# Weights laid side by side in the prologue of an attention and state-space kernel

## The chip, the cores and the metric

The kernel runs on one core of one Trainium2 chip. The metric is the device time of one execution, in microseconds (us). TensorE (PE) multiplies, VectorE (DVE), ScalarE (ACT) and GpSimd (POOL) do the element-wise work, and SyncE (SP) issues nearly all transfers.

## The reference

Two independent halves are computed and set side by side in the output. Half A is a state-space layer over a sequence of 2048 steps with 640 channels; half B is attention with 32 query heads of 20 elements that share one key head and one value head.

```
B:  q = (x @ wq) in 32 heads of 20     k = x @ wk      v = x @ wv
    p = softmax(q k^T / sqrt(20))      b = (p v, heads joined) @ wo
A:  h[t] = Lam_bar * h[t-1] + x[t] @ B_bar^T           (complex, 640 states)
    a = 2 Re(h @ C^T) + x * Dskip
out = concatenate([a, b])              x is (1, 2048, 640), bfloat16
```

## The kernel before, in words

**Tiling.** The scores of one head group (4 heads), one block of 512 queries and one chunk of 128 keys make a tile of 128 keys by 512 queries; there are 4 query blocks x 8 head groups x 16 key chunks x 4 heads = 2048 such tiles. A score tile is one product with a contraction over 32 rows (20 elements of the head, one row that carries a bound, the rest zero). Its exponential is made in one of two ways. ACT exponentiates two or three tiles in one instruction (line 1457, out tile PR, shapes 128x1024 and 128x1536). Or DVE turns one tile into the bits of a bfloat16 number by an addition and a conversion to integers (line 862, out tile BIG, 128x512), and three more integer additions, on DVE (line 862, BIG from BIG) or on POOL (line 1772, two tiles at once), make shifted copies of it that take part in the weighted sum too. The sums over keys (MB from PR,VP and MB from BIG,VS) are PE products of 32 columns each, four of them beside one another in the four column strips of the array.

**Order.** Nothing of the order is written by hand. `Schedule` (line 46) is a list scheduler that runs while the program is built: each step has an engine, a planned duration, dependences and a priority, and whichever ready step has the lowest priority number goes next on its engine. Sources such as `fill` (line 1394) and `pv_source` (line 1785) decide at the planned time which tile goes to ACT and which to DVE. `planned` (line 505) makes 32 such plans with small random shifts, and keeps the one that it believes shortest. So a changed duration, priority or step early in the program changes what is decided later, up to the end. `Emitter.plan` (line 271) then turns dependences into semaphore waits. Each engine runs its own stream strictly in order.

**The prologue** ends when the first exponential starts on ACT. Its steps:

- `loads` (line 1013): SP issues, in this order, the first two blocks of B's x (tile CT), the first 80 columns of wq, three transposing loads of the third and fourth block of x into BIG (tile xbT in the code; the fourth block in two parts of 3 and 2 chunks), wv, the rest of wq, and the two matrices B_re and B_im (tile BA, 800 KB each). wk goes out on ACT's queue.
- `kv_steps` (line 1094): `turn` transposes the first two blocks on PE (line 725, SC from ident,CT), and DVE or ACT copies the result to BIG (lines 1110 and 1113). `kv` makes the keys of each of the four blocks `tb`. The 20 columns of wk are wanted in four copies, one for each of the four row groups of the score product, so each of the 5 chunks of the contraction is multiplied four times by the same 32 columns, once for each column strip (`four`, line 1227): 20 products of 128x32 weights per block, tile wkr. DVE then takes the largest absolute value of each row (line 1130, tile mab), and ACT copies the keys to KT (line 1136).
- `bound` (line 1154): from the maxima of the first three blocks DVE makes `Mp` (lines 1156 and 861); when the fourth arrives, one combined instruction makes M0 (line 1161, tile M). The maximum over all four (line 1164) goes to DRAM (mrep, line 705) and comes back spread over the partitions (mcol); DVE then makes Mm from it (line 857), from which the bounds of the remaining head groups come.
- `qt_task` (line 1235) makes the queries of the first head group: a first product with zeros (MB from PR,VZ) and then, for each of 5 chunks, four products of 20 columns of wq (MB from BIG). ACT copies them to QT (line 1252), DVE takes absolute values (line 861), a product with M0 adds the bound (MB from BIG,M), and DVE writes QT again (line 862, QT from MB,lift). Then the first scores can be made.
- `warm_source` (line 933) fills idle time of PE in the prologue with products of zeros (MB from PR).

**Just after the start**, PE makes the rest of the queries (line 795, SC from BIG) and values (`v_task`, line 1183: lines 1187 and 1195) in banks that are lent by the two sets of three score banks (SC0, SC1). DVE, in its stream order, copies these, scales the state-space matrices (BA, CA), waits for mcol, and makes Mm. Until a lent bank has been emptied by DVE, the set that lent it can't take its third tile.

Of the kernel before, what the change touches and what calls it, by code (L numbers as in the profile page):

```python
# [12 lines left out]
ALU = mybir.AluOpType  # L13
AX = mybir.AxisListType
FP32 = mybir.dt.float32
BF16 = mybir.dt.bfloat16
# [449 lines left out]
class Build:  # L466
# [191 lines left out]
    def alloc_early(self, s):  # L658
        self.maskM = self.sb(s, "maskM", [128, NC, 32], FP32)
        self.mask0 = self.sb(s, "mask0", [128, 4, 32], FP32)  # L660
        self.Mp = self.sb(s, "Mp", [128, 4, 32], FP32)
# [6 lines left out]
        self.EARLY = ["iota", "one", "vrow", "maskM", "mask0", "Mp", "turn2", "angc"] + [f"early_fr{c}{i}" for c in range(NC) for i in range(2)]  # L668

# [348 lines left out]
    def loads(self):  # L1018
# [23 lines left out]
        self.wq_op = L(wqd[:, :, 80:640], wqv[:, :, 80:640], 380000, "wq", strided=True, writes=["wqb"])  # L1042
        for o, t in zip(self.vec_op + self.xn_op + [self.wk_op, self.wqa_op, self.wv_op, self.wq_op], self.LANDS):
            o.lands = t
# [54 lines left out]
    def kv_steps(self):  # L1099
# [20 lines left out]
        def kv(tb):  # L1120
            yield lambda: all((tb, c) in self.xb_op for c in range(NC)) and (tb < self.PLAIN or self.s.done([self.xb_op[tb, 0]])) \
                and any(x in self.early for x in self.free_banks)
            bank = self.take(self.early)
            prev = None
            for c in range(NC):
                prev = self.pe(self.four(bank, [p.wkr[:, c, :]] * 4, p.xbT[:, c, 512 * tb:512 * tb + 512], c == 0, c == NC - 1),
                               self.mmt(512), mode="C", prio=self.KP if tb < 3 else 1.15,
                               deps=[self.xb_op[tb, c], self.wk_op] + bank.last, prev=prev,
                               reads=[f"xbT{tb}_{c}", "wkr"], writes=[bank.key])
            red = self.dve(lambda e, src=bank.ap: e.tensor_reduce(out=p.mab[:, tb:tb + 1], in_=src, axis=AX.X, op=ALU.max,  # L1130
                                                     apply_absolute_value=True), 650, deps=[prev], reads=[bank.key],
                           writes=[f"mab{tb}"], prio=0.31)
            self.red_op[tb] = red
            dst, src = p.KT[:, 512 * tb:512 * tb + 512], bank.ap
            if self.KEYS[tb] == "a":
                kt = self.act(lambda e: e.activation(dst, src, ACT.Identity, bias=p.lift[:, 2:3], scale=ALPHA * UNIT), 600,
                              deps=[red, self.lift_op], reads=[bank.key, "lift"], writes=[f"KT{tb}"], prio=0.34)
            else:
                kt = self.dve(self.ts(dst, src, ALPHA * UNIT, p.lift[:, 2:3], ALU.mult, ALU.add), 640,
                              deps=[red, self.lift_op], reads=[bank.key, "lift"], writes=[f"KT{tb}"], prio=0.44)  # L1140
            self.kt_op[tb] = kt
            yield lambda: kt.start is not None
            bank.last = [kt]
            self.give(bank)
            if tb < 2:
                yield lambda: any(x in self.early for x in self.free_banks)
                yield from self.v_task(tb, self.take(self.early))
# [6 lines left out]
        def bound():  # L1154
            yield lambda: set(range(3)) <= set(self.red_op)
            most = self.dve(lambda e: e.tensor_reduce(out=p.mab[:, 6:7], in_=p.mab[:, 0:3], axis=AX.X, op=ALU.max), 120,
                            deps=[self.red_op[i] for i in range(3)], reads=[f"mab{i}" for i in range(3)], writes=["mabp"], prio=0.32)
            low = self.dve(self.ts(p.Mp[:], p.mask0[:], p.mab[:, 6:7], None, ALU.mult), 200, port=True,
                           deps=[most, self.c_op["mask0"]], reads=["mabp", "mask0"], writes=["Mp"], prio=0.32)
            yield lambda: len(self.red_op) == 4  # L1160
            self.m0_op = self.dve(lambda e: e.scalar_tensor_tensor(out=p.M0[:], in0=p.mask0[:], scalar=p.mab[:, 3:4], in1=p.Mp[:],
                                                                   op0=ALU.mult, op1=ALU.min), 250,
                                  deps=[self.red_op[3], low, self.c_op["mask0"]], reads=["mab3", "Mp", "mask0"], writes=["M0"], prio=0.3)
            m = self.dve(lambda e: e.tensor_reduce(out=p.mab[:, 4:5], in_=p.mab[:, 0:4], axis=AX.X, op=ALU.max), 120,
                         deps=[self.red_op[3]], reads=[f"mab{i}" for i in range(4)], writes=["mabs"],
                         prio=0.36)
            many = bass.AP(tensor=p.mab, offset=4, ap=[[8, DH], [0, H], [1, 1]])
            out = self.load(p.mrep.rearrange("(h d o) -> d h o", d=DH, o=1), many, 2560, "mo", strided=True, deps=[m], reads=["mabs"],
# [38 lines left out]

    def take(self, which=None):
        for b in self.free_banks:
# [17 lines left out]
    def four(self, bank, lhs, rhs, start, stop):  # L1227

        return [self.mm(bank.tensor[32 * j:32 * j + lhs[j].shape[-1], bank.off:bank.off + 512], lhs[j], rhs, start, stop,
                        tile_position=(0, 32 * j), skip_group_check=True) for j in range(4)]  # L1230

    def first_made(self):
        return (0, -1) in self.half_op and self.half_op[0, -1][0].start is not None

    def qt_task(self, bank, g=0):

        p = self
        rank = self.QR if g == 0 else 1.3
        prev = self.pe(self.four(bank, [p.VZ[:]] * 4, p.PR[:, 0, :] if g == 0 else p.KT[:, 0:512], True, False), self.mmt(512),
                       deps=[self.c_op["VZ"], self.zero_op] + bank.last + ([self.kt_op[0]] if g else [self.wqa_op]), prio=rank, mode="C",  # L1240
                       reads=["VZ", "KT0" if g else "PR0"], writes=[bank.key])
        for c in range(NC):
            at = 640 * c + 80 * g
            prev = self.pe(self.four(bank, [p.wqf[:, at + 20 * j:at + 20 * j + 20] for j in range(4)], p.xbT[:, c, 0:512],
                                     False, c == NC - 1), self.mmt(512), deps=[self.wqa_op, self.wq_op][:g + 1] + [self.xb_op[0, c]],
# [793 lines left out]
    def ssm_scalars(self):  # L2039
# [23 lines left out]
        def ts(o, a, s1, s2, op0, op1=None):  # L2063
# [7 lines left out]
        w = self.pe([self.mm(bank.cols(16, 16 + NC), p.vrow[:], p.ident[0:4 * NC, 3 * NC:4 * NC], True, True)], 80.0,  # L2071
                    deps=[self.vec_op[3], v, chain[0]], reads=["ident"] + [f"vrow{i}" for i in range(4)], writes=[bank.key], prio=1.06)
        skip = self.dve(lambda e: e.tensor_copy(sc[:, 3, :], bank.cols(16, 16 + NC)), 150, deps=[w], reads=[bank.key], writes=["scd"],
# [35 lines left out]
        for lo, hi in ((0, 3), (3, NC)):  # L2109
            keys = [f"early_fr{c}{i}" for c in range(lo, hi) for i in range(2)]  # L2110
            t = self.act(lambda e, lo=lo, hi=hi: e.activation(p.tab[:, lo:hi, 1:3, :], p.fr[:, lo:hi].bitcast(I16)[:, :, :, 0::2], ACT.Sin,
                                                              scale=TWO_PI / 65536.0), 200 + 427 * (hi - lo), table="sin",
                         deps=turns[2 * lo:2 * hi] + [sin_table], reads=keys, writes=[f"tab{c}" for c in range(lo, hi)], prio=0.4, gate=self.turned)
            tabs += [t] * (hi - lo)
# [438 lines left out]
```

## Time and profile before

| what | value |
|---|---|
| median of 3 runs (lowest, highest) | 710.6 us (709.87, 711.77) |
| time of the profiled execution | 711.06 us |
| its span on the core | 709.2 us |
| ACT busy | 693.6 us |
| PE busy | 688.4 us |
| DVE busy | 610.4 us |
| POOL busy | 467.3 us |
| first exponential starts on ACT | 19.15 us |

The profiled execution's own time is 1.86 us longer than its span; this stands before the first and behind the last instruction. Busy time of PE is modelled from overlapping products and is no measure of how much room PE has. In lines of groups the columns are: line, engine, operation, output from inputs, shapes and count; then busy time and mean duration of one in ns; then idle time of the engine before them and what ended it.

### The profile page before, as it was taken

How to read it: one execution, taken by the hardware profiler on the slowest of the kernel's cores; microseconds unless marked ns; L12 is line 12 of the kernel's file. 1: busy time of each engine (PE TensorE's matmuls, PEld its weight loads, DVE VectorE, ACT ScalarE, POOL GpSimd, SP SyncE). 2: the span in 40 equal slices, each digit the busy share in tenths (PEclk: the TensorE clock that was granted, in tenths of full speed). 3: DMA queues.
4: the chain of work that ended last, by engine and by line, in shares of the span. 5: the costliest groups of instructions: out<-in, count | busy, mean ns of one | idle time of the engine just before them, and what ended most of it. 6: DMA issues, size and time to landing. Idle time of an engine off the chain costs nothing.

```text
span 709.2 us, 26838 instructions
## 1 busy us (share of the span) xinstructions
PE 688.4 (97%) x11287; PEld 246.0 (35%) x11287; DVE 610.4 (86%) x1168; ACT 693.6 (98%) x703; POOL 467.3 (66%) x796
## 2 busy tenths in 40 slices
PE   8999999999999999999999999999999999999997
PEld 4322323434333533333433333334233333342323
DVE  7899899987897788888789999889999997987783
ACT  6899999999999999999999999999999999999996
POOL 4255673046697566955757776967867777798881
PEclk9999999999999999999999999999999999999999
DMA  9687652120120000100301000120000001110001
GB/s 208 152 170 164 139 106 78 37 48 11 27 66 10 21 21 22 50 22 17 65 10 37 19 18 25 49 61 20 10 17 20 14 25 31 31 28 16 26 15 39
DMA packets 77588, 34.44 MB, mean 49 GB/s; under 512 B 58350, under 2 KB 77470, under 8 KB 77470
## 3 DMA queue, kind: packets, MB, share of 16 engines
q1 hardware_dynamic: 76506, 32.44, 19.8%
q8 instruction: 90, 1.47, 0.9%
q10 hardware_dynamic: 964, 0.29, 0.2%
q14 instruction: 28, 0.23, 0.1%
HBM read 11.53 MB, written 9.75 MB: 30 GB/s over the span
## 4 chain that ended last, share of the span: by engine, by line
ACT 49%; PE 44%; DMA 3%; DVE 2%; SPq 1%; issue 0%; DVEq 0%
ACT PR L1457 49%; PE MB L725 17%; PE MB L795 11%; PE SC L725 11%; PE MB L805 4%; DMA mrep<-mab 2%; SPq L710 1%; DMA BIG<-in_B_x_dram 1%; DVE BIG L862 1%; PE MB L721 1%; DMA mcol<-mrep 1%; PE SC L721 0%; DMA qd<-BIG 0%; SPq L706 0%; DVE prod L857 0%
## 5 line engine op out<-in xcount | busy, mean ns | idle before, releaser
L1457 ACT ACTIVATE PR<-SC 128x1024 bf16<-128x1024 f32 (+1 forms) x681 | 679.4, 1197 | 4.0 <-PE SC L725 2.8
L1772 POOL INT64_ADD BIG<-BIG x762 | 455.4, 614 | 214.3 <-DVE BIG L862 118.7
L862 DVE TENSOR_SCALAR BIG<-SC 128x512 int16<-128x512 f32 x529 | 356.3, 685 | 67.7 <-PE SC L725 60.8
L725 PE MATMUL SC<-QT,KT 32*128 32x512 bf16 x2013 | 266.4, 384 | 10.3 <-ACT PR L1457 5.2
L725 PE MATMUL MB<-BIG,VS 128*32 128x512 bf16 x2256 | 247.8, 384 | 0.3 <-DVE pvsb L1839 0.2
L725 PE MATMUL MB<-PR,VP 128*32 128x512 bf16 x1484 | 204.9, 384 | 0.0
L725 PEld LDWEIGHTS SC<-QT,KT 32*128 32x128 bf16 x2013 | 68.1, 90 | 174.2 <-ACT PR L1457 113.1
L725 PEld LDWEIGHTS MB<-BIG,VS 128*32 128x32 bf16 x2256 | 59.1, 94 | 61.4 <-issue 39.1
L725 PEld LDWEIGHTS MB<-PR,VP 128*32 128x32 bf16 x1484 | 49.9, 94 | 49.5 <-issue 36.5
L795 PE MATMUL MB<-CT,W 128*32 128x320 bf16 (+2 forms) x1000 | 53.4, 301 | 0.4 <-DVE prod L857 0.2
L805 PE MATMUL MB<-xaT,BT 32*128 32x256 bf16 x184 | 35.6, 272 | 1.6 <-ACT PR L1457 1.4
L862 DVE TENSOR_SCALAR BIG<-BIG 128x1024 int16<-128x1024 int16 (+1 forms) x91 | 34.7, 410 | 2.6 <-PE MB L725 2.3
L795 PE MATMUL MB<-CA,W 128*32 128x512 bf16 (+1 forms) x640 | 35.2, 302 | 0.3 <-DVE prod L857 0.2
L795 PE MATMUL MB<-xaT,BA 128*32 128x256 bf16 x800 | 32.0, 275 | 0.1
L805 PE MATMUL MB<-diagD,xaT 32*128 32x128 bf16 x320 | 31.3, 217 | 0.0
L795 PEld LDWEIGHTS MB<-CT,W 128*32 128x32 bf16 x1000 | 22.8, 96 | 15.2 <-issue 6.6
L805 PEld LDWEIGHTS MB<-diagD,xaT 32*128 32x128 bf16 x320 | 17.7, 92 | 28.4 <-ACT PR L1457 20.4
L795 PE MATMUL MB<-xaT,BT 128*32 128x256 bf16 x616 | 26.1, 274 | 0.0
L857 DVE TENSOR_TENSOR prod<-MB,tab 128x1024 bf16<-128x1024 f32 x20 | 24.3, 1215 | 0.5 <-PE SC L725 0.5
L2024 DVE CAST stg<-MB 128x512 bf16<-128x512 f32 x35 | 23.8, 679 | 1.1 <-PE MB L795 0.8
L862 DVE TENSOR_SCALAR BIG<-MB 128x512 int16<-128x512 f32 x35 | 23.8, 680 | 0.0
L795 PE MATMUL MB<-WO,OP 128*32 128x128 bf16 (+1 forms) x480 | 23.5, 302 | 0.0
(167 smaller groups left out, 469.5 us busy)
## 6 DMA issues: line engine op xcount, KB each, us to landing
out_dram<-stg SPq DMA_DIRECT2D x31, 128.0 KB, 1.9
qd<-BIG SPq DMA_DIRECT2D x20, 128.0 KB, 2.2
QT<-qd SPq DMA_DIRECT2D x28, 80.0 KB
OP<-pvsb SPq DMA_DIRECT2D x105, 20.0 KB
rdP<-recs SPq DMA_DIRECT2D x105, 20.0 KB
lbd<-BA SPq DMA_DIRECT2D x5, 320.0 KB, 3.3
CT<-in_B_x_dram SPq DMA_DIRECT2D x2, 640.0 KB, 5.3
BA<-in_A_B_re_dram SPq DMA_DIRECT2D x1, 800.0 KB, 7.1
```

The lines of the kernel that those rows point to most:

```text
L710: fns = [lambda e, o=o, i=i: e.dma_start_transpose(o, i) for o, i in pairs]
L721: r = e.matmul(out[32 * j:32 * j + 32], lhsT=lhsT[:, 32 * j:32 * j + 32], rhs=rhs, start=start, stop=stop, tile_position=(0, 32 * j), skip ...
L725: return lambda e: e.matmul(out, lhsT=lhsT, rhs=rhs, start=start, stop=stop, **kw)
L795: x = e.matmul(out[32 * j:32 * j + 32], lhsT=lhsT[:, 32 * j:32 * j + 32], rhs=rhs, start=start, stop=r.end is tag, tile_position=(0, 32 * ...
L805: return lambda e: e.matmul(out, lhsT=lhsT[at], rhs=rhs[at], start=False, stop=r.end is tag, tile_position=(32 * row, 0), skip_group_check ...
L857: return lambda e: e.tensor_tensor(out, a, b, op)
L862: return lambda e: e.tensor_scalar(out, a, s1, s2, op0=op0, op1=op1)
L1457: ex = self.act(lambda e: e.activation(dst, t[:, 0:512 * n], ACT.Exp, scale=1.0 / UNIT), 0.8333 * 512 * n + 64, table="exp", deps=[op], re ...
L1772: op.fns.append(lambda e: e.int64_add(words(dst), words(src), add))
L2024: ev = self.dve(lambda e: e.tensor_copy(st, bank.ap), 645, deps=[prev], reads=[bank.key], writes=[key], prio=self.EV, gate=(lambda: last.e ...
```

## The change

Three things are changed in the prologue, with the constants that belong to them.

1. **Weights side by side.** POOL copies wk's padded 32 columns four times beside one another into a new tile `wks` (128 columns per chunk), and the 80 columns of wq of the first head group into `wqp` with 12 zeros between the heads (DVE clears the tile first). For the second, third and fourth block one product with 128 columns then makes what four products with 32 columns made; for the first head group's queries too, without the first product with zeros. The first block keeps its four products (`QUAD_KEYS = 1`).
2. **Last keys in halves.** The fourth block is multiplied in two halves of 256 columns, in the order `KEY_STEPS`: chunks 0 to 2 of both halves (they land first), then chunks 3 and 4 of the one half and of the other. Each half has its own maximum.
3. **The bound as one maximum and one product.** `Mp` and the combined instruction go; DVE takes the maximum of the five maxima and multiplies the mask by it.

Priorities of the key products, of the sine and of one small product are changed, the first block's keys are copied by DVE in place of ACT, and the banks of the prologue are taken in a given order (`KEY_BANKS`).

```diff
+        again = bass.AP(tensor=p.wkr, offset=0, ap=[[NC * 32, 128], [32, NC], [0, 4], [1, 32]])
+        spread = p.wks[:].rearrange("p (c j n) -> p c j n", c=NC, j=4)
+        self.wks_op = self.pool(lambda e: e.tensor_copy(spread, again), 800, deps=[self.wk_op], reads=["wkr"], writes=["wks"],
+                                prio=self.WKP, port=True)
...
+        zero = self.dve(lambda e: e.memset(p.wqp[:], 0.0), 170, writes=["wqp"], prio=0.65)
+        self.wqp_op = self.pool(lambda e: e.tensor_copy(padded, dense), 600, deps=[zero, self.wqa_op], ...)
...
-    PLAIN, KP, QR, FRP = 2, 1.1, 1.12, 0.36
-    TURNED, KEYS = ("dadad", "dadad"), "aaaa"
+    PLAIN, KP, QR, FRP, SINP, SKIP_P, KEY_BANKS = 2, (1.04, 1.04, 1.06, 1.08), 1.05, 0.36, 0.32, 1.03, "2543016"
+    WKP, QUAD_KEYS = 0.9, 1
+    TURNED, KEYS = ("dadad", "dadad"), "daaa"
...
-            for c in range(NC):
-                prev = self.pe(self.four(bank, [p.wkr[:, c, :]] * 4, p.xbT[:, c, 512 * tb:512 * tb + 512], c == 0, c == NC - 1),
+            parts = 1 if tb < 3 else 2
+            n = 512 // parts
+            steps = [(x, c) for x in range(parts) for c in range(NC)] if tb < 3 else self.KEY_STEPS
+            for x, c in steps:
+                at = 512 * tb + n * x
+                if tb < self.QUAD_KEYS:
+                    prev = self.pe(self.four(bank, [p.wkr[:, c, :]] * 4, p.xbT[:, c, at:at + 512], c == 0, c == NC - 1), ...
+                else:
+                    prev = self.pe([lambda e, x=x, c=c, at=at: e.matmul(bank.cols(n * x, n * x + n), lhsT=p.wks[:, 128 * c:128 * c + 128],
+                                                                        rhs=p.xbT[:, c, at:at + n], start=c == 0, stop=c == NC - 1, ...
+                if c == NC - 1:
+                    red = self.dve(... tensor_reduce(out=to, in_=src, axis=AX.X, op=ALU.max, apply_absolute_value=True), 115 + 1.05 * n, ...
...
-            low = self.dve(self.ts(p.Mp[:], p.mask0[:], p.mab[:, 6:7], None, ALU.mult), 200, port=True, ...
-            self.m0_op = self.dve(lambda e: e.scalar_tensor_tensor(out=p.M0[:], in0=p.mask0[:], scalar=p.mab[:, 3:4], in1=p.Mp[:],
-                                                                   op0=ALU.mult, op1=ALU.min), 250, ...
+            yield lambda: len(self.red_op) == 5
+            m = self.dve(lambda e: e.tensor_reduce(out=p.mab[:, 5:6], in_=p.mab[:, 0:5], axis=AX.X, op=ALU.max), 120, ...
+            self.m0_op = self.dve(self.ts(p.M0[:], p.mask0[:], p.mab[:, 5:6], None, ALU.mult), 200, port=True, ...
...
+    KEY_STEPS = ((0, 0), (0, 1), (0, 2), (1, 0), (1, 1), (1, 2), (0, 3), (0, 4), (1, 3), (1, 4))
...
+            if g == 0:
+                prev = self.pe([lambda e, c=c: e.matmul(bank.ap, lhsT=p.wqp[:, 128 * c:128 * c + 128], rhs=p.xbT[:, c, 0:512], ...
```

More of the change, by code (lines that the diff above doesn't have):

```diff
@@ L667, in alloc_early @@
         self.vrow = self.sb(s, "vrow", [20, 128], BF16)
-        self.EARLY = ["iota", "one", "vrow", "maskM", "mask0", "Mp", "turn2", "angc"] + [f"early_fr{c}{i}" for c in range(NC) for i in range(2)]
+        self.wqp = self.sb(s, "wqp", [128, NC * 128], BF16)
+        self.wks = self.sb(s, "wks", [128, NC * 128], BF16)
+        self.EARLY = ["iota", "wqp", "wks", "one", "vrow", "maskM", "mask0", "turn2", "angc"] + [f"early_fr{c}{i}" for c in range(NC) for i in range(2)]
     def alloc_late(self, s):
@@ L1122, in kv @@
                 and any(x in self.early for x in self.free_banks)
[L1123 removed]
+            bank = self.take(self.early, self.KEY_BANKS)
             prev = None
[L1125 to L1129 removed]
@@ new lines, in kv @@
+            for x, c in steps:
+                at = 512 * tb + n * x
+                if tb < self.QUAD_KEYS:
+                    prev = self.pe(self.four(bank, [p.wkr[:, c, :]] * 4, p.xbT[:, c, at:at + 512], c == 0, c == NC - 1), self.mmt(512),
+                                   mode="C", prio=self.KP[tb], deps=[self.xb_op[tb, c], self.wk_op] + bank.last, prev=prev,
+                                   reads=[f"xbT{tb}_{c}", "wkr"], writes=[bank.key])
+                else:
+                    prev = self.pe([lambda e, x=x, c=c, at=at: e.matmul(bank.cols(n * x, n * x + n), lhsT=p.wks[:, 128 * c:128 * c + 128],
+                                                                        rhs=p.xbT[:, c, at:at + n], start=c == 0, stop=c == NC - 1,
+                                                                        skip_group_check=True)],
+                                   self.mmt(n), prio=self.KP[tb], deps=[self.xb_op[tb, c], self.wks_op] + bank.last, prev=prev,
+                                   mode="F", load=float(n), reads=[f"xbT{tb}_{c}", "wks"], writes=[bank.key])
+                if c == NC - 1:
+                    red = self.dve(lambda e, src=bank.cols(n * x, n * x + n), to=p.mab[:, tb + x:tb + x + 1]: e.tensor_reduce(
+                        out=to, in_=src, axis=AX.X, op=ALU.max, apply_absolute_value=True), 115 + 1.05 * n, deps=[prev], reads=[bank.key],
+                        writes=[f"mab{tb + x}"], prio=0.31 if x == parts - 1 else 0.315)
+                    self.red_op[tb + x] = red
@@ L1146, in kv @@
                 yield lambda: any(x in self.early for x in self.free_banks)
-                yield from self.v_task(tb, self.take(self.early))
+                yield from self.v_task(tb, self.take(self.early, self.KEY_BANKS))
             else:
@@ L1154, in bound @@
         def bound():
[L1155 to L1167, printed above, removed]
+            yield lambda: len(self.red_op) == 5
+            m = self.dve(lambda e: e.tensor_reduce(out=p.mab[:, 5:6], in_=p.mab[:, 0:5], axis=AX.X, op=ALU.max), 120,
+                         deps=list(self.red_op.values()), reads=[f"mab{i}" for i in range(5)], writes=["mabs"], prio=0.3)
+            self.m0_op = self.dve(self.ts(p.M0[:], p.mask0[:], p.mab[:, 5:6], None, ALU.mult), 200, port=True,
+                                  deps=[m, self.c_op["mask0"]], reads=["mabs", "mask0"], writes=["M0"], prio=0.3)
+            many = bass.AP(tensor=p.mab, offset=5, ap=[[8, DH], [0, H], [1, 1]])
             out = self.load(p.mrep.rearrange("(h d o) -> d h o", d=DH, o=1), many, 2560, "mo", strided=True, deps=[m], reads=["mabs"],
@@ L1206, in v_task, with take @@
         self.give(bank)
-    def take(self, which=None):
-        for b in self.free_banks:
+    def take(self, which=None, order=None):
+        for b in self.free_banks if order is None else sorted(self.free_banks, key=lambda b: order.find(b.key[1])):
             if which is None or b in which:
@@ L2071, in ssm_scalars @@
         w = self.pe([self.mm(bank.cols(16, 16 + NC), p.vrow[:], p.ident[0:4 * NC, 3 * NC:4 * NC], True, True)], 80.0,
-                    deps=[self.vec_op[3], v, chain[0]], reads=["ident"] + [f"vrow{i}" for i in range(4)], writes=[bank.key], prio=1.06)
+                    deps=[self.vec_op[3], v, chain[0]], reads=["ident"] + [f"vrow{i}" for i in range(4)], writes=[bank.key], prio=self.SKIP_P)
         skip = self.dve(lambda e: e.tensor_copy(sc[:, 3, :], bank.cols(16, 16 + NC)), 150, deps=[w], reads=[bank.key], writes=["scd"],
```

23 lines of the change are left out of this document (14 added, 9 removed).

## The prediction

> **What bounds the kernel now.** First the page: which engine ends the work, and what its main groups are.
>
> ```profile
> ACT 49%; PE 44%; DMA 3%; DVE 2%; SPq 1%; issue 0%; DVEq 0%
> L1457 ACT ACTIVATE PR<-SC 128x1024 bf16<-128x1024 f32 (+1 forms) x681 | 679.4, 1197 | 4.0 <-PE SC L725 2.8
> ```
>
> The chain names ACT and PE nearly alike, so I ask who waits for whom. The waits, and ACT's timeline at the start and at the end:
>
> ```profile
> PEld SC L725 <- ACT PR L1457: 113.1, 277, 0.8
> ...
> PEld SC L725 <- DVE BIG L862: 33.8, 77, 0.8
> ...
> 19.15 12.94 ACT L1457 ACTIVATE PR<-SC 128x1024 bf16<-128x1024 f32 x14 [1.53 <-PE SC L725]
> 33.32 167.29 ACT L1457 ACTIVATE PR<-SC 128x1024 bf16<-128x1024 f32 x159 [1.23 <-PE SC L725]
> ...
> 696.21 4.84 ACT L1457 ACTIVATE PR<-SC 128x1536 bf16<-128x1536 f32 x4
> 701.71 0.60 ACT L1844 ACTIVATE pvsb<-MB 128x512 bf16<-128x512 f32 x1 [0.66 <-PE MB L725]
> ```
>
> PE's score products wait for ACT for 113 us; ACT's exponentials are idle for 4.0 us. ACT is the bound from 19.15 to 701.05 (696.21 + 4.84). The shapes apart:
>
> ```profile
> L1457 ACT ACTIVATE PR<-SC 128x1024 bf16<-128x1024 f32 x557 | 524.2, 1111 | 3.9 <-PE SC L725 2.8
> L1457 ACT ACTIVATE PR<-SC 128x1536 bf16<-128x1536 f32 x123 | 175.6, 1592 | 0.1
> L1457 ACT ACTIVATE PR<-SC 128x512 bf16<-128x512 f32 x1 | 0.8, 847 | 0.0
> ```
>
> Instructions overlap, so I take their spacing: two tiles (12.94 - 1.11) / 13 = 0.910 us, three (4.84 - 0.85) / 3 = 1.33 us. 557 x 0.910 + 123 x 1.33 + 0.85 = 671.3 us of the 681.9 us. Of the other 10.6 us, 1.23 us are one gap at 32 us and 9.3 us are small delays spread over the run. Last, what sets the start and this gap, from the chain of the first 60 us in order of time (start, length):
>
> ```profile
> 10.09 5.40 DMA BIG<-in_B_x_dram
> ...
> 15.53 0.64 PE SC L725 x8
> ...
> 16.20 0.70 DVE mab L1130
> ...
> 16.93 0.35 DVE M L1161
> ...
> 17.38 10.94 DMA mrep<-mab
> ...
> 28.33 3.79 DMA mcol<-mrep
> ...
> 32.14 0.33 DVE Mm L857
> ```
>
> The last piece of x lands at 15.49 us, whatever PE does. The maximum then takes a way of 14.7 us through DRAM, and DVE stands still for it until 32.14 us.
>
> **The change part by part.**
>
> *Fewer products.* Neighbours in the timeline for the new forms:
>
> ```profile
> 11.40 1.26 PE L725 MATMUL SC<-BIG,wkr 128*32 128x512 bf16 x20 [0.16 <-DMA BIG<-in_B_x_dram]
> ...
> 16.08 0.39 PE L725 MATMUL MB<-PR 128*128 128x512 bf16 x1
> ...
> 17.73 1.04 PE L725 MATMUL MB<-PR 128*128 128x512 bf16 x4
> ```
>
> Twenty strip products take 1.26 us, because four run beside one another. Full products follow at (1.04 - 0.39) / 3 = 0.217 us, with 0.39 for one alone, so five take 4 x 0.217 + 0.39 = 1.26 us too. Instructions go, time doesn't; the zero product saves 0.2 us in a stretch where PE waits for transfers anyway. I count 0.
>
> *The copies.* POOL makes `wks` once wk has landed, `wqp` once the first columns of wq have, and only then the last three additions for the sine and the clearing of VS.
>
> ```profile
> 2.80 0.38 SPq L705 DMA_DIRECT2D BIG<-in_B_wq_dram  x1
> 6.30 1.14 POOL L2106 INT64_ADD fr<-fr  x3 [1.86 <-DVE fr L862]
> 9.32 1.80 POOL L1005 MEMSET VS<- 128x2048 bf16 x1
> ...
> BIG<-in_B_wq_dram SPq DMA_DIRECT2D x1, 100.0 KB, 5.6
> ```
>
> No row shows a POOL copy. The nearest clears 2048 columns in 1.80 us, so 400 columns are 0.35 us if they scale, and 1.80 us at the most; I take 0.6, nearer to the lower end, since a copy reads as well. From landing at 2.80 + 5.6 = 8.4: 0.6 + 1.14 + 1.80 gives 11.9 us (13.1 at the upper end). DVE's small fills of VS wait for that, and in DVE's order the maxima of the last halves stand behind; those start at about 15.9 us, so at least 2 us of cover is left. I count 0; if the cover is gone, each us late is one us later at the first exponential. The Trainium skill, GPSIMD Engine Reference, section Elementwise, gives 769 ns for 512 elements in a tight loop of these cores, by which 400 columns are, as an estimate, also 0.6 us. A copy's pattern with gaps isn't among its cases, and no run so far shows it.
>
> *Halves and bound.* Rows for DVE's new steps:
>
> ```profile
> 13.44 0.16 DVE L1156 TENSOR_REDUCE mab<-mab 128x1 f32<-128x3 f32 x1
> 13.63 0.29 DVE L861 TENSOR_SCALAR Mp<-mask,mab 128x128 f32<-128x128 f32 x1
> ```
>
> From 15.53: two products of 256 columns (0.11 apart, half of 0.217; 0.3 for the last, under the 0.39 of a long one) end at 15.94. A maximum over 256 columns lies between 0.16 and 0.70 us; I take the middle, 0.43. The halves run 15.98 to 16.41 and on to 16.84, the maximum of five 0.16, the mask's product 0.29: done at 17.3 us. Before, M was done at 16.93 + 0.35 = 17.28. What the halves win, the added serial step takes. I count 0 (-0.3 to +0.3).
>
> *And it wouldn't matter.* The second stage is pinned by a transfer, not by the start:
>
> ```profile
> BA<-in_A_B_im_dram SPq DMA_DIRECT2D x1, 800.0 KB, 13.8
> 14.35 0.53 SPq L706 DMA_DIRECT2D BA<-in_A_B_im_dram  x1
> ...
> 32.59 0.23 DVE L1195 CAST VP<-SC 128x80 bf16<-128x80 f32 x1
> 32.86 0.49 DVE L857 TENSOR_TENSOR VS<-VP,vsc 128x320 bf16<-128x320 bf16 x1
> 32.88 0.39 PE L725 MATMUL SC<-QT,KT 32*128 32x512 bf16 x3 [1.50 <-DVE VP L1195]
> 33.27 0.48 DVE L857 TENSOR_TENSOR BA<-BA,CA 128x640 bf16<-128x640 bf16 x1
> 33.67 0.68 DVE L862 TENSOR_SCALAR BIG<-SC 128x512 int16<-128x512 f32 x1
> ...
> 34.74 0.69 DVE L1279 CAST BIG<-SC 128x512 bf16<-128x512 f32 x1
> ...
> 35.34 0.54 DVE L862 TENSOR_SCALAR CA<-BA,sc 128x1280 bf16<-128x1280 bf16 x1
> ```
>
> mrep lands at 28.3, just behind BA at 14.35 + 13.8 = 28.15, on SP's queue; in the new order SP issues the same list up to there. So mcol lands at 32.1 again. What stands behind Mm on DVE differs. Before, the copy of VP did, so ACT had 14 exponentials behind it and resumed at 33.32. In the new order VP is ahead of Mm, and two more pairs can run. The 17th fill waits for DVE's first exponential, which stands behind Mm, VS, a copy of a few columns (as the small maximum, 0.16) and two products on BA: 32.41 + 0.45 + 0.16 + 2 x 0.5 + 0.68 = 34.75, plus PE's 0.4 and the hand-over: 35.27 us. Before, that exponential would have been due at 33.32 + 2 x 0.91 = 35.14: +0.13. The 18th waits for two further DVE steps (0.54 and 0.69), so until 35.98, and PE's 0.4 and the hand-over make 36.47 where 35.27 + 0.91 was due: +0.29; a later one about +0.1. Together +0.5. It is 0 if DVE catches up, +1.0 if each step slips.
>
> *The redrawn plan.* All that follows is planned anew. Counted in the instruction order of the changed kernel, ACT has 552 two-tile and 125 three-tile exponentials and no single one: 1479 tiles in place of 1484. The sum is 552 x 0.910 + 124 x 1.33 + 1.59 = 668.8, against 671.3: **-2.5 us**. Five tiles go to DVE. Stretches between two fills with more than 4.5 rounds of four products, the ones that make ACT late, are 50 in place of 55, so I leave the 9.3 us as they are, +-1.5. The tail behind the last exponential has the same chain of steps.
>
> **Sum**: 0 + 0.5 - 2.5 = -2.0 us. Against the profiled execution, 711.06 - 2.0 = 709.1 us; that execution stood 0.46 above the median of 710.6, which would give 708.6. I take 709.0.
>
> **The rivals.**
>
> *A, ACT's saved work comes back as waiting.* The chain's 44% for PE, and a PE that does the same weighted sums, speak for it; PE's 113 us of waiting for ACT speak against. Then the time is that of before plus the +0.5: about 711.
>
> *B, the stall at 32 us goes too.* If mcol lands about 1.5 us earlier, say because its first leg, issued some 0.4 us earlier, no longer sits behind BA, neither order waits: -2.5 - 1.23 - 0.3 for the start, about 707. Against it stands that both legs follow BA's issue on one queue.
>
> *C, slower: DVE becomes the bound.* The rows:
>
> ```profile
> L862 DVE TENSOR_SCALAR BIG<-SC 128x512 int16<-128x512 f32 x529 | 356.3, 685 | 67.7 <-PE SC L725 60.8 <-PE MB L725 1.4 <-POOL BIG L1772 1.0
> L862 DVE TENSOR_SCALAR BIG<-BIG 128x1024 int16<-128x1024 int16 x77 | 31.0, 428 | 2.3 <-PE MB L725 1.9
> 519.00:619.00 100.00, 98.75 (x1528) 33.14 (x1524) 93.10 (x165) 99.67 (x104) 74.38 (x125) 1.00 0.09 24
> ```
>
> In the new order DVE gets five more exponentials and 101 double copies in place of 77 (and five single ones fewer); POOL gives up 14. That is 5 x 0.685 + 24 x 0.428 = 13.7 us more for DVE, 2.0 us per 100 us, where it is busy 93.1 already (third busy figure). It decides from the point where the sets' third tiles come free too late, the wait of 33.8 us above. If half of the 13.7 us reaches ACT: 711.06 - 2.0 + 6.9 = 716; a quarter, 712.5. Against it: 95 of 100 still leaves room. The Trainium skill, SBUF — State Buffer, section SBUF: two separate sides, says that GpSimd and some DVE operations shut each other out of a shared port for a whole instruction; more copies on DVE would then hold up POOL's too, which no row here separates.
>
> *D, the change doesn't do what it says.* For PE's time this is my forecast: fewer instructions, the same time.
>
> **How the numbers follow.** Forecast (707.8 to 710.2) 0.45, A (to 712.4) 0.22, B 0.14, C 0.19. The measurement can tell about 0.3%, 2.1 us, from no change: faster means under 708.5, slower over 712.7. Faster: B and half of the forecast, 0.36. Slower: nearly all of C, 0.17. The rest, 0.47, is the same. The range takes in B's 706.5 and C up to 713.5.
>
> **What would show it.** Right: the first exponential at 19.0 to 19.3 us; mcol landing near 32.1; a gap of ACT near 34 to 35 in place of 32; 677 exponentials on ACT at the same spacings; small delays of ACT near 9 us. Wrong: POOL's copies ending behind 14 us; ACT idle that names DVE all along the run (C); no gap at all before 40 us (B); delays of 12 us or more (A).

## The result, and the profile after

The changed kernel takes 708.9 us (median of 11 runs, 707.4 to 709.94), the kernel before, run beside it, 711.27 us (median of 11, 709.28 to 715.05): ratio 0.9957, with a 95% interval of 0.9938 to 0.9976. It is faster by 0.4%. By the bound that the prediction set (faster means under 708.5) this would still count as no change; the interval, from executions side by side, leaves out 1. The profiled execution took 708.9 us with a span of 707.2 us, 2.0 less than the span of before.

The page of the kernel after, its chain by engine and ACT's exponentials by shape:

```profile
ACT 56%; PE 36%; DVE 4%; SPq 1%; DMA 1%; issue 1%; POOL 1%; DVEq 0%; POOLq 0%
...
L1481 ACT ACTIVATE PR<-SC 128x1024 bf16<-128x1024 f32 x552 | 519.5, 1106 | 3.9 <-PE SC L726 2.9 <-PE MB L726 0.6
L1481 ACT ACTIVATE PR<-SC 128x1536 bf16<-128x1536 f32 x125 | 178.4, 1564 | 0.4 <-PE MB L726 0.2 <-PE SC L726 0.2
```

ACT's timeline after, exponentials only:

```profile
19.38 24.93 ACT L1481 ACTIVATE PR<-SC 128x1024 bf16<-128x1024 f32 x27 [1.61 <-PE SC L726]
44.46 13.92 ACT L1481 ACTIVATE PR<-SC 128x1536 bf16<-128x1536 f32 x14 [0.16 <-PE SC L726]
58.63 277.33 ACT L1481 ACTIVATE PR<-SC 128x1536 bf16<-128x1536 f32 x268 [0.25 <-PE MB L726]
...
675.00 23.83 ACT L1481 ACTIVATE PR<-SC 128x1024 bf16<-128x1024 f32 x23 [0.19 <-PE SC L726]
```

ACT runs from 19.38 to 698.83 (675.00 + 23.83): 679.45 us in place of 681.9. At the spacings of the prediction its work is 668.8 in place of 671.3, so the rest (the time from the first to the last exponential, less that work) is 10.6 us in both. But it is not the same 10.6: before, 1.23 of it was the gap at 32 us. Now there is no gap (27 exponentials run through from 19.38 to 44.31), and the small delays have grown from 9.4 (9.3 in the prediction's rounding) to 10.6. The start is 0.23 later, and what lies behind the last exponential is 8.3 us long in place of 8.2.

DVE's rows after, from the last keys to the bound, and around Mm:

```profile
16.29 0.76 DVE L1152 TENSOR_REDUCE mab<-SC 128x1 f32<-128x256 f32 x2 [2.24 <-PE SC L1146]
17.08 0.16 DVE L1178 TENSOR_REDUCE mab<-mab 128x1 f32<-128x5 f32 x1
17.27 0.29 DVE L862 TENSOR_SCALAR M<-mask,mab 128x128 bf16<-128x128 f32 x1
...
30.32 0.23 DVE L1210 CAST VP<-SC 128x80 bf16<-128x80 f32 x1
30.67 0.32 DVE L858 TENSOR_TENSOR Mm<-maskM,mcol 128x160 bf16<-128x160 f32 x1
```

Mm starts at 30.67, with no wait for mcol, in place of 32.14 behind a wait of 1.64 us. The last part of x landed at 15.59 (15.49 before); M was done at 17.56 (17.28 before).

### The profile page after: what moved, and what is told of

The parts are those of the page before. It is cut to its first block, busy times and chain, and to the rows that moved or that the text cites. A ratio compares the mean times of both kernels' runs of the same rounds, so it can differ in the third digit from the quotient of the medians.

```text
span 707.2 us, 26738 instructions
## 1 busy us (share of the span) xinstructions
PE 689.4 (97%) x11235; PEld 247.7 (35%) x11235; DVE 621.2 (88%) x1193; ACT 690.3 (98%) x698; POOL 462.4 (65%) x784
## 4 chain that ended last, share of the span: by engine, by line
ACT 56%; PE 36%; DVE 4%; SPq 1%; DMA 1%; issue 1%; POOL 1%; DVEq 0%; POOLq 0%
ACT PR L1481 56%; PE MB L726 13%; PE MB L796 10%; PE SC L726 8%; PE MB L806 4%; DVE BIG L863 2%; SPq L711 1%; PE SC L796 1%; DMA BIG<-in_B_x_dram 1%; POOL BIG L1796 1%; PE SC L722 0%; DVE prod L858 0%; DVE BIG L1303 0%; SPq L707 0%; DVE stg L2048 0%
## 5 line engine op out<-in xcount | busy, mean ns | idle before, releaser
L1796 POOL INT64_ADD BIG<-BIG x748 | 449.3, 617 | 216.3 <-DVE BIG L863 102.7
L726 PE MATMUL MB<-BIG,VS 128*32 128x512 bf16 x2276 | 256.8, 384 | 0.0
L726 PE MATMUL MB<-PR,VP 128*32 128x512 bf16 x1479 | 216.8, 384 | 0.0
L726 PEld LDWEIGHTS MB<-BIG,VS 128*32 128x32 bf16 x2276 | 61.3, 94 | 65.5 <-issue 42.0
L726 PEld LDWEIGHTS MB<-PR,VP 128*32 128x32 bf16 x1479 | 52.6, 94 | 44.5 <-issue 31.8
L863 DVE TENSOR_SCALAR BIG<-BIG 128x1024 int16<-128x1024 int16 (+1 forms) x110 | 42.0, 417 | 4.4 <-PE MB L726 4.2
L806 PE MATMUL MB<-xaT,BT 32*128 32x256 bf16 x176 | 34.0, 272 | 1.3 <-ACT PR L1481 1.1
L806 PEld LDWEIGHTS MB<-diagD,xaT 32*128 32x128 bf16 x320 | 17.7, 92 | 28.4 <-ACT PR L1481 17.3
```

The costliest lines, as they stand in the source:

```text
L726: return lambda e: e.matmul(out, lhsT=lhsT, rhs=rhs, start=start, stop=stop, **kw)
L806: return lambda e: e.matmul(out, lhsT=lhsT[at], rhs=rhs[at], start=False, stop=r.end is tag, tile_position=(32 * row, 0), skip_group_check ...
L863: return lambda e: e.tensor_scalar(out, a, s1, s2, op0=op0, op1=op1)
L1796: op.fns.append(lambda e: e.int64_add(words(dst), words(src), add))
```

## The experiments

Three theories. **1**: the gain is the redrawn plan; the edits that give the change its name buy nothing. **2**: the gain is the new prologue. **3**: the gain is the gap at 32 us. The table has one traced execution of each run, its start and rest read as above (us), and beside it the median and the ratio to the kernel before, which was run beside each. The traced execution need not be near the median: that of a_s131 took 714.63 us.

| run | last of x lands | first exp. | ACT's work | rest | span | median | ratio (95% interval) |
|---|---|---|---|---|---|---|---|
| before | 15.49 | 19.15 | 671.3 | 10.6 | 709.2 | | |
| b_again | 15.61 | 19.27 | 671.3 | 8.95 | 707.7 | one run, 709.53 | |
| a_old | 14.59 | 19.90 | 671.3 | 8.95 | 708.3 | 710.64 | 0.9997 (0.9979, 1.0015) |
| b_bim | 15.38 | 19.04 | 671.3 | 14.9 | 713.5 | 714.06 | 1.0049 (1.0028, 1.0071) |
| b_sin | 15.51 | 19.41 | 668.8 | 10.85 | 707.2 | 709.03 | 0.9968 (0.9947, 0.9988) |
| after | 15.59 | 19.38 | 668.8 | 10.6 | 707.2 | 708.9 | 0.9957 (0.9938, 0.9976) |
| a_strips | 15.96 | 19.77 | 668.8 | 10.4 | 707.3 | 708.34 | 0.9970 (0.9956, 0.9983) |
| a_whole | 14.15 | 18.67 | 668.8 | 9.7 | 705.6 | 708.88 | 0.9972 (0.9953, 0.9991) |
| a_2bank | 15.69 | 19.26 | 668.8 | 10.5 | 706.6 | 708.36 | 0.9957 (0.9939, 0.9975) |
| a_s131 | 14.48 | 20.04 | 673.4 | 10.6 | 712.8 | 712.89 | 1.0031 (1.0011, 1.0052) |
| a_s31 | 15.46 | 19.25 | 666.7 | 13.0 | 708.7 | 710.63 | 0.9994 (0.9974, 1.0013) |
| a_s82 | 14.24 | 18.38 | 667.5 | 11.0 | 705.4 | 708.49 | 0.9964 (0.9940, 0.9988) |
| a_2b141 | 15.53 | 19.09 | 668.3 | 9.4 | 704.7 | 707.04 | 0.9942 (0.9922, 0.9963) |

In a_old and a_s131 x landed early and the first exponential came late all the same. PE was behind there: it began to transpose the first block at 7.53 and 7.36 us (5.75 in the kernel after), behind seven products with zeros that took 3.17 us in place of 2.29. The steps up to there are the same in all three, so this belongs to the execution, not to the edit.

**One constant (b_sin).**

```diff
-    ..., writes=[f"tab{c}" for c in range(lo, hi)], prio=0.4, gate=self.turned)
+    ..., writes=[f"tab{c}" for c in range(lo, hi)], prio=0.32, gate=self.turned)
```

> The kernel before with one constant changed: the priority of the sine of ACT is 0.32 in place of 0.4. None of the new products, copies, halves or bound. With this alone the instruction order behind the prologue is that of the changed kernel (552 two-tile and 125 three-tile exponentials, 1479 tiles, in place of 557, 123 and 1 single, 1484). Theory 1 (the gain is the redrawn plan): 2.0 to 2.5 us under the kernel before, ratio about 0.997. Theory 2 (the gain is the new prologue): no change, ratio 1.000. Theory 3 (the gain is the gap of 1.23 us at 32 us): ratio 1.000 if ACT still idles more than 1 us there, 0.998 if not.

709.03 us, ratio 0.9968 (0.9947 to 0.9988). The kernel before, with not one of the new instructions, takes the time of the kernel after when the sine's priority is changed (the intervals overlap; a difference of 0.1% between the two is not excluded). From the first exponential on, the traces of both show the same steps in the same order on ACT, DVE and POOL. ACT's timeline of this run has the rows of after, 0.1 us later:

```profile
19.41 25.04 ACT L1457 ACTIVATE PR<-SC 128x1024 bf16<-128x1024 f32 x27 [1.77 <-PE SC L725]
44.60 13.92 ACT L1457 ACTIVATE PR<-SC 128x1536 bf16<-128x1536 f32 x14 [0.16 <-PE SC L725]
```

Theory 2 falls as the main cause.

**All edits, old priorities (a_old).**

```diff
-    PLAIN, KP, QR, FRP, SINP, SKIP_P, KEY_BANKS = 2, (1.04, 1.04, 1.06, 1.08), 1.05, 0.36, 0.32, 1.03, "2543016"
+    PLAIN, KP, QR, FRP, SINP, SKIP_P, KEY_BANKS = 2, (1.1, 1.1, 1.1, 1.15), 1.12, 0.36, 0.4, 1.06, None
```

> The changed kernel with all its new products, copies, halves and bound, but with the old priorities and the old choice of banks. Its plan then belongs to the other family: over the 32 plans that are drawn ACT gets 1485 tiles on average, as in the kernel before, where the changed kernel's plans get 1480. Theory 1: the gain is gone, ratio 0.999 to 1.002. Theory 2: the gain stays, ratio about 0.997. First exponential for both at 19.2 to 19.5 us.

710.64 us, ratio 0.9997 (0.9979 to 1.0015): the gain is gone. The order from the start of the exponentials on is that of the kernel before. With b_sin this makes a table of two by two: the old plan takes the same with either prologue, the new plan gains with either. It also speaks against theory 3 as the main cause: this trace has no gap at 32 us, and the median is no lower.

**Strips again (a_strips).** Each new product is issued as four strips, put in after the planning so that nothing else moves. In short, for the keys:

```diff
-    e.matmul(bank.cols(n * x, n * x + n), lhsT=p.wks[:, 128 * c:128 * c + 128], rhs=p.xbT[:, c, at:at + n], ...)
+    [e.matmul(bank.tensor[32 * j:32 * j + 32, bank.off + n * x:bank.off + n * x + n], lhsT=p.wkr[:, c, :],
+              rhs=p.xbT[:, c, at:at + n], ..., tile_position=(0, 32 * j), ...) for j in range(4)]
```

> The changed kernel with its instruction order kept to the last instruction, but each full product of 128 columns in the prologue (20 of the keys, 5 of the queries) is issued again as four strip products of 32 columns, 75 instructions of PE more. Theory 1: nothing changes, first exponential within 0.2 us of 19.38, ratio to the kernel before about 0.997. Theory 2: the first exponential comes 0.5 us or more later, and the time is up by as much or more, ratio 0.998 to 1.000.

708.34 us, ratio 0.9970 (0.9956 to 0.9983). The first exponential missed its band (19.77, 0.39 later), because x landed 0.37 later in this execution: 3.81 us behind the landing, and 3.79 in the kernel after. PE's rows of the last keys, with strips and then in the kernel after:

```profile
16.00 0.62 PE L1155 MATMUL SC<-BIG,wkr 128*32 128x256 bf16 x16 [1.59 <-DMA BIG<-in_B_x_dram]
```

```profile
15.64 0.61 PE L1146 MATMUL SC<-BIG,wks 128*128 128x256 bf16 x4 [1.66 <-DMA BIG<-in_B_x_dram]
```

Sixteen strips and four full products take the same.

**B_im behind mcol (b_bim).** In the order of the kernel before, one load is moved (`bn1` is B_im, `mi` the issue of mcol). In short:

```diff
+    order = em.order
+    op = order.pop(next(k for k, o in enumerate(order) if o.dma_key == "bn1"))
+    order.insert(1 + next(k for k, o in enumerate(order) if o.dma_key == "mi"), op)
```

> The kernel before, all orders kept but one: on SP's queue the load of B_im stands behind the issue of mcol, not ahead of mrep. Theory 3 (the maximum's way through DRAM sits behind the 800 KB of B_im, and makes the gap of 1.23 us at 32 us): mrep lands before 23 us and mcol before 26 us, the gap is under 0.3 us, and the time is down by 1.2 us, ratio about 0.998. Rival: mcol comes early, but the copies that DVE still has to make take the gap's place, or the scaling of the matrices waits for B_im: ACT still idles about 1 us between 30 and 40 us, ratio 1.000.

714.06 us, ratio 1.0049 (1.0028 to 1.0071), slower, and a surprise as well. From its chain of the first 60 us:

```profile
17.26 9.09 DMA mrep<-mab
...
26.77 5.42 DMA BA<-in_A_B_im_dram
```

And what DVE waited for, and with it ACT:

```profile
32.22 0.56 DVE L869 TENSOR_SCALAR CA<-BA,sc 128x1280 bf16<-128x1280 bf16 x1 [4.12 <-DMA BA<-in_A_B_im_dram]
```

```profile
36.25 1.02 ACT L1464 ACTIVATE PR<-SC 128x1024 bf16<-128x1024 f32 x1 [3.44 <-PE SC L732]
37.76 1.02 ACT L1464 ACTIVATE PR<-SC 128x1024 bf16<-128x1024 f32 x1 [0.48 <-PE SC L732]
39.28 1.03 ACT L1464 ACTIVATE PR<-SC 128x1024 bf16<-128x1024 f32 x1 [0.50 <-PE SC L732]
```

mrep's way is 9.09 us with no B_im on the queue, in place of 10.94 with it in the kernel before. But with B_im ahead it took anything from 8.6 to 12.4 us over the other traces, so most of the way is its own, and this one pair gives no price for B_im. Since SP waits for mrep before it issues mcol, B_im is now issued at 26.77 and lands at 32.19, and DVE's scaling stands still for it for 4.12 us; ACT then for 3.44. The waits of half a microsecond behind that have another cause. PE had nothing to do from 31.56 to 34.62 us, and the granted clock of TensorE fell. PE's rows, and the stretches of this trace, where the clock is the third figure from the end:

```profile
34.62 1.04 PE L802 MATMUL SC<-BIG 128*32 128x512 bf16 x8 [3.06 <-DVE BIG L1286]
35.60 0.61 PE L732 MATMUL SC<-QT,KT 32*128 32x512 bf16 x3
...
40.38 0.39 PE L732 MATMUL SC<-QT,KT 32*128 32x512 bf16 x3
```

```profile
30.00:32.00 2.00, 1.56 (x26) 0.61 (x18) 0.00 (x0) 2.00 (x4) 0.00 (x0) 1.00 1.08 386
32.00:34.00 2.00, 0.00 (x0) 0.00 (x0) 1.64 (x6) 0.81 (x1) 0.00 (x0) 0.82 1.29 268
34.00:40.00 6.00, 5.38 (x43) 1.00 (x44) 4.50 (x13) 2.77 (x3) 0.00 (x0) 0.50 0.63 100
40.00:42.00 2.00, 2.00 (x27) 0.50 (x19) 2.00 (x5) 1.49 (x3) 0.61 (x1) 0.97 0.41 127
```

At a clock of 0.50 three score products take 0.61 us in place of 0.39, and ACT waits 0.48 to 0.51 us three times more. In the kernel before PE waited 1.50 us at this place, and the clock stayed at 1.00. The first half of the expectation failed (mrep at 26.35, not before 23), the rival came true in its second form. A wait of DVE near 32 us does reach the end, and with it the slower PE behind it: the span is 4.3 us longer than before.

**The kernel before, a second trace (b_again).**

> The kernel before once more, for a second trace. Theory: the gap of ACT at 32 us goes by when mcol lands, which differs from run to run. If it lands at 31 us or later, the gap is there again, with 10.0 to 10.5 us between the work and the time from the first to the last exponential; if it lands before 29.5 us, there is no gap and these are 9.2 us or less, as in the run a_old. Rival: a gap of 1 us or more whenever mcol lands.

One run of 709.53 us. mcol landed at 29.27 in place of 32.12, Mm had not to wait, and ACT had no gap:

```profile
19.27 43.22 ACT L1457 ACTIVATE PR<-SC 128x1024 bf16<-128x1024 f32 x46 [1.53 <-PE SC L725]
```

The rest is 8.95 us, as in a_old, where mcol landed at 28.77. (a_old starts 0.63 us later than this run, and its span is 0.6 longer: a later start passes to the end in full.) So the gap that the prediction took for a property of the kernel is one of the execution. In the new order mcol landed between 29.2 and 32.2 us, and in the latest of these, a_strips, Mm started at 32.26 and ACT still had no gap behind it:

```profile
28.34 17.10 ACT L1491 ACTIVATE PR<-SC 128x1024 bf16<-128x1024 f32 x18 [0.21 <-PE SC L730]
```

VP is copied ahead of Mm there, as the prediction had seen, and that is cover enough.

The landing of mcol moves with that of B_im. The rows of the earliest and the latest trace in which SP stood waiting for mrep behind it, a_old and then a_strips:

```profile
13.56 0.53 SPq L707 DMA_DIRECT2D BA<-in_A_B_im_dram  x1
26.19 0.36 SPq L706 DMA_DIRECT2D mcol<-mrep  x1
BA<-in_A_B_im_dram SPq DMA_DIRECT2D x1, 800.0 KB, 11.8
```

```profile
14.61 0.55 SPq L711 DMA_DIRECT2D BA<-in_A_B_im_dram  x1
30.10 0.37 SPq L710 DMA_DIRECT2D mcol<-mrep  x1
BA<-in_A_B_im_dram SPq DMA_DIRECT2D x1, 800.0 KB, 15.0
```

B_im lands at 25.3 and 29.6 us, and mcol is issued, which is when mrep has landed, 0.2 to 0.9 us behind it in all eleven such traces. Whether mrep waits for B_im or both for the same thing is not shown; b_bim says only that without B_im mrep is not there before 26.35 us either.

**Other plans (a_s131, a_s31, a_s82).** The changed kernel, with one random shift of the planner given by hand:

```diff
-        for seed in range(self.PLANS):
+        for seed in (131,):
```

> The changed kernel with another of the small random shifts of its planner: all steps, priorities and the prologue are the same, but the order behind it is drawn anew, here with 552 two-tile, 128 three-tile exponentials and 1 single one on ACT, 1489 tiles in place of 1479. Theory 1 (ACT's sum of work sets the time): 552 x 0.910 + 127 x 1.33 + 1.59 + 0.85 = 673.7 in place of 668.8, so 4.9 us over the changed kernel, ratio to the kernel before about 1.004. Rival: the time goes by the waits that a plan makes, not by ACT's sum, and these fall when DVE has ten tiles fewer: under 2 us over the changed kernel, ratio under 1.000.

712.89 us, ratio 1.0031 (1.0011 to 1.0052); 4.0 us over the 708.9 of the kernel after, and 4.5 over a_2bank (708.36), which has the plan of after and was run beside it. Expected were 4.9; by the table's work it is 4.6, since a single exponential ends this plan and the expectation counted a longer one at the end as well. The same prologue, the same edits, and the time is above that of before: theory 1, once more.

> As the run before, with a shift that gives ACT 557 two-tile and 120 three-tile exponentials, 1474 tiles. Theory 1, by ACT's sum alone: 557 x 0.910 + 119 x 1.33 + 1.59 = 666.7, so 2.1 us under the changed kernel, ratio to the kernel before about 0.994. Rival: with five tiles more on DVE and POOL, ACT waits for them, and the time is that of the changed kernel or more, ratio 0.997 to 1.000.

710.63 us, ratio 0.9994 (0.9974 to 1.0013). Here the rival holds: ACT has 2.1 us less to do, and its rest is 2.3 us longer, its end behind the last exponential 1.4. ACT's rows name who it waits for:

```profile
L1481 ACT ACTIVATE PR<-SC 128x1024 bf16<-128x1024 f32 x557 | 524.9, 1110 | 4.4 <-PE SC L726 2.9 <-PE MB L726 1.2
L1481 ACT ACTIVATE PR<-SC 128x1536 bf16<-128x1536 f32 x120 | 172.8, 1565 | 2.4 <-PE MB L726 2.2 <-PE SC L726 0.2
```

The waits for the weighted sums (MB) are 3.4 us in place of 0.8. So theory 1 stands with a limit: ACT's sum of work is what a plan can gain, and the waits that the plan makes can take all of it back.

> As the two runs before, with a shift that gives ACT 552 two-tile and 124 three-tile exponentials, 1476 tiles. Theory 1, by ACT's sum alone: 552 x 0.910 + 123 x 1.33 + 1.59 = 667.5, so 1.3 us under the changed kernel, ratio to the kernel before about 0.995. Rival, as for the run before: 0.997 or more.

708.49 us, ratio 0.9964 (0.9940 to 0.9988), between the two expectations: not told apart.

**Halves in two banks, and no halves (a_2bank, a_whole).** In the kernel after the first half's maximum stands still until the last product of the second half. Both halves write one bank, and `Emitter.plan` keeps account by bank. a_2bank gives the second half a bank of its own (`two`, the second of SC0), put in after the planning; a_whole has no halves. In short:

```diff
-    e.matmul(bank.cols(n * x, n * x + n), lhsT=p.wks[:, 128 * c:128 * c + 128], ...)
+    e.matmul(two.cols(0, n), lhsT=p.wks[:, 128 * c:128 * c + 128], ...)
...
-            parts = 1 if tb < 3 else 2
+            parts = 1
```

> The changed kernel with its order kept, but the second half of the last keys is multiplied into another bank of PSUM (the second of SC0, which is free), so that the first half's maximum no longer has to wait for the last product of the second half; ACT copies the last keys in two pieces of 256 columns. Theory H (in the changed kernel the halves cannot overlap, because they share a bank and the first maximum therefore waits for all four last products): the first maximum starts 0.25 to 0.3 us earlier after the landing of the last part of x, and so does the first exponential, 3.5 us behind the landing in place of 3.8 (19.38 less 15.59). Time down by the same 0.3 us at most, ratio to the kernel before 0.996 to 0.997. Rival: the copy in two pieces or DVE's next steps take it back, 3.8 us or more.

> The changed kernel with the last keys whole: five products of 512 columns, one maximum over 512, and the maximum of four in place of five. Theory H (in one bank the halves win nothing): the first exponential comes 3.7 to 3.8 us behind the landing of the last part of x, as with the halves (3.79). Rival (the halves are worth about half a maximum as they stand): 4.1 us or more. The plan behind it is the same, so the ratio to the kernel before stays at 0.996 to 0.997 with either.

DVE's rows of a_2bank, where x landed at 15.69:

```profile
16.16 0.42 DVE L1163 TENSOR_REDUCE mab<-SC 128x1 f32<-128x256 f32 x1 [2.00 <-PE SC L1153]
16.51 0.41 DVE L1168 TENSOR_REDUCE mab<-SC 128x1 f32<-128x256 f32 x1
```

The first maximum now starts 0.47 us behind the landing (0.70 in the kernel after), the first exponential 3.57 (3.79): 0.22 us, a little under the 0.25 to 0.3 expected. The total is 708.36, ratio 0.9957 (0.9939 to 0.9975); a gain of that size is not to be seen in it. a_whole gave no answer by its measure: x landed at 14.15, before PE was through with the earlier keys, so 4.5 us behind the landing says nothing of halves. From the start of the last maximum to M it took 15.20 to 16.40, 1.20 us; with halves in one bank 16.29 to 17.56, 1.27. In one bank the halves win nothing.

**A version under both (a_2b141).** a_2bank with the shift 141:

> Try for a version under both kernels: the second half of the last keys in a bank of its own, as in the run a_2bank, and another of the small random shifts of the planner, which gives ACT 566 two-tile and 115 three-tile exponentials, 1477 tiles: 566 x 0.910 + 114 x 1.33 + 1.59 = 668.3, 0.5 under the changed kernel. If its small delays and its end are those of the changed kernel (10.6 and 8.3 us): 0.7 us under it, ratio to the kernel before 0.995. Rival (a plan with more on DVE gives it back in waits, as in the run a_s31): 0.997 or more.

707.04 us (median of 12), ratio 0.9942 (0.9922 to 0.9963), under the kernel before by 0.6%. The work is as counted, the rest 9.4. Against the kernel after (0.9957) the intervals overlap, so this much is not shown: that it is the faster of the two.

## Why the prediction was right

The forecast of 709.0 us came out, and its main term, five tiles fewer on ACT in a redrawn plan, was right. Three smaller terms failed, and their errors cancelled: that the total is met within 0.1 us is luck. Of the signs that the prediction named for itself only the 677 exponentials came as said. The first exponential (19.38 us), mcol (29.48), the gap near 34 to 35 and the small delays near 9 us did not, and a sign against it did come: no gap before 40 us, which it had given to rival B.

- **Fewer products: 0.** Right (a_strips). The copies were hidden as worked out: POOL's rows after:

```profile
6.88 0.72 POOL L1035 COPY wks<-wkr 128x640 bf16<-128x640 bf16 x1
8.91 0.52 POOL L1051 COPY wqp<-BIG 128x400 bf16<-128x400 bf16 x1 [1.32 <-DVE fr L863]
9.41 1.14 POOL L2130 INT64_ADD fr<-fr  x3
10.50 1.80 POOL L1006 MEMSET VS<- 128x2048 bf16 x1
```

  0.52 us where 0.6 was taken, and VS clear at 12.3 where 11.9 was. The estimate by the Trainium skill, GPSIMD Engine Reference, section Elementwise, was 0.6 too, and the row agrees within 0.1.
- **Halves and bound: 0.** Missed by 0.2 us, within the 0.3 allowed: M done at 17.56, not 17.3, with x landing 0.1 later. The step that failed is "The halves run 15.98 to 16.41 and on to 16.84": the first maximum waits for all four last products, since both halves share a bank (a_2bank).
- **The stall at 32 us, +0.5.** Wrong, the sign too. The step that failed is "So mcol lands again at 32.1": that mrep lands just behind B_im held in all eleven traces in which SP waited for it, but B_im's landing, 28.1 us in one trace, was taken for fixed. It lay between 25.3 and 29.6 us, and mcol landed anywhere from 28.5 to 32.2 us over all traces, in the kernel before too (b_again). In the profiled pair the gap went (-1.23), which is rival B's effect by chance of execution. The gaps that the prediction put at 34 to 35 us did not come, even with Mm at 32.26. (Its sum for the 17th fill makes 34.70, not 34.75; nothing hangs on that.)
- **The plan, -2.5.** Right as ACT's sum: 668.8 against 671.3.
- **Small delays, 0 (within 1.5).** They grew by 1.3 us in the profiled pair (9.36 to 10.62 before rounding), near the end of what was allowed, and by 1.7 against the undisturbed traces of the old plan (8.95 to 10.6), so rival A was partly true. The new plan's net gain where no gap disturbs the old is 2.5 - 1.7 = 0.8 us; with the gap it is 2.0.
- **Over many executions.** b_sin's medians say 1.2 us (710.26 for the kernel before beside it, 709.03), and its ratio, into which every execution enters, 2.3. What lies between are executions with a lower granted clock. Of the 35 executions of the kernel before beside b_sin nine show a mean clock of 0.992 to 0.998, and these took 711.5 to 716.3 us; the other 26, at 0.999 or 1.0, have a median of 709.94, 0.9 over b_sin. None of the twelve of b_sin is under 0.999, and none of the 57 of all kernels with the plan of after (b_sin, after, a_strips, a_whole, a_2bank). So about half of the 2.3 is ACT's shorter work, less the waits; the other half is that such executions do not come. b_bim, with a mean of 0.995, shows one way to them: a longer wait near 32 us, and then 0.50 for six microseconds. That the late executions of the kernel before had a late mcol and such a wait fits, but none of them was traced.
- **Rival C.** DVE did get more to do, 621.2 us busy in place of 610.4, without becoming the bound.

Sum of the profiled pair: start +0.23, plan -2.5, gap -1.23, small delays +1.3, end +0.15: -2.05, and the spans say -2.0. The prediction had 0, -2.5, +0.5, 0 and 0.

What stays open: why the earlier sine leads to plans with fewer tiles on ACT. Over the 32 plans that are drawn, ACT gets 1485.0 on average in the kernel before, 1480.0 with the sine at 0.32. The traces show only where it begins. DVE's exponentials begun in the first 60 us, in a_old and in b_sin:

```profile
L863 DVE TENSOR_SCALAR BIG<-SC 128x512 int16<-128x512 f32 x13 | 8.9, 684 | 0.2
L863 DVE TENSOR_SCALAR BIG<-MB 128x512 int16<-128x512 f32 x5 | 3.4, 683 | 0.0
```

```profile
L862 DVE TENSOR_SCALAR BIG<-SC 128x512 int16<-128x512 f32 x20 | 13.4, 683 | 0.1
L862 DVE TENSOR_SCALAR BIG<-MB 128x512 int16<-128x512 f32 x2 | 1.4, 692 | 0.0
```

They are 18 and 22. Open as well is why B_im lands so differently from one execution to the next.

## What to carry to other kernels

Where a planner decides the order, undo the constants and the edits separately before you credit an edit: here one priority gave the gain, as far as the intervals can tell. Count a changed plan in the bound engine's instructions, but price its waits as a term of their own, for against traces without the gap they took back 1.7 us of the 2.5 that the count promised. And do not call a wait a property of the kernel from one trace: run the kernel before a second time and see whether it is still there.

## What the runs showed of the hardware

- The write of the maximum, 640 pieces of 4 bytes, took 9.09 us to land in b_bim, where B_im was not yet on its queue (B_re, ahead of it, had landed at 20.5 us), and 8.6 to 12.4 us over all traces; the read of the same 2.5 KB took 2.1 to 3.8. The Trainium skill, Perfetto Trace Analysis, section Per-instruction lifecycle, says that the semaphore's update waits until the write is completed, which "can cause a surprisingly long delay especially when the write target is HBM". The traces agree in direction (9.09 us for the write in b_bim, 2.1 for the read); no run took the small pieces and the target apart.
- The last part of x landed at 14.15 to 15.96 us, though it was issued between 10.0 and 10.2 us in every run. Where it landed early (14.15 to 14.59, in four traces), PE was the limit. PE's rows of a_s82, x at 14.24:

```profile
12.92 2.33 PE L1146 MATMUL SC<-BIG,wks 128*128 128x512 bf16 x15
...
15.77 0.91 PE L1202 MATMUL SC<-wvr,BIG 128*128 128x20 bf16 x30
16.62 0.40 PE L726 MATMUL MB<-BIG,M 128*32 128x512 bf16 x4
```

The keys run without a break to 15.25, and the first exponential came at 18.38. Only in such executions could the new prologue pay; no trace of the old prologue with an early landing is there to compare.

- PE without work for 3.06 us was followed by a granted clock of 0.50 for six microseconds (b_bim, 34 to 40 us), without work for 1.50 us by none (the kernel before, 1.00 throughout). Where between the two the clock begins to fall no run shows.
